# A fused linear attention and two MLPs on one core: the second MLP in five super blocks of 960 and 896 tokens and not in six of 768

## The chip, the core and the metric

The kernel runs on one core of a Trainium2 chip. The metric is the device time of one execution in microseconds (us), from the first to the last instruction with what lies around it. PE is the matmul engine, DVE, ACT and POOL are the three engines for elementwise work, SP issues nearly all DMAs. Each engine works through its own instructions in order; a semaphore makes one wait for another.

## The reference

The attention is linear: q is normalised over the head dimension, k over the sequence, and q is multiplied by the small matrix k'v of its head. Its output, 4608 tokens of 512, goes through two MLPs of width 2048.

```python
kv = einsum('bhsd,bhse->bhde', k_s, v)          # k_s: softmax of k over the sequence
attn = einsum('bhsd,bhde->bhse', q_s, kv)       # q_s: softmax of q over the head dimension
x = attn.transpose(0, 2, 1, 3).reshape(4608, 512)
h = x @ w_in;   x = maximum(h, 0) ** 2 @ w_out                    # first MLP
h = x @ w_in2;  out = (h / (1 + exp(-1.702 * h))) @ w_out2        # second MLP
```

## The kernel before

**Number format.** Every fp32 matmul is made of three with operands split in a high and a low part (`three`, L1193): high x high, high x low, low x high. The high part is a copy on ACT (L634), the low part a difference on POOL or DVE (L637).

**First part.** Attention and the first MLP run over nine blocks of 512 tokens, until about 867 us. Their matmuls are 512 columns wide, later (from the fourth block) a mix of 256 and 512.

**The second MLP** runs over `NB2` = 6 super blocks of 768 tokens. Both of its matrix products are made by a scheme of seven half-size products in place of eight (Winograd's form of Strassen's), so a super block is cut in two halves of `TH` = 384 tokens, and 384 is the width of all its matmuls. Each super block i does this:

- `steps_s` (L1456) loads the tokens into one tile (`xf`) and makes seven forms of it, a11, s2, a12, s3, s1, a22, s4: sums and differences of its quarters, each with high and low part. They lie in a ring of ten places, `X_PLACES` (L1422): three tiles of `xpool` and seven pairs or thirds of others.
- `steps_l1` (L1522) runs n = 8i to 8i + 7, with two blocks of 128 hidden units each. Every n has seven **products** of six matmuls, in the order a11, s2, a12, s3, s1, a22, s4, into two PSUM banks by turns. DVE and ACT take the results out, add, apply the activation and make seven forms of g (named ga and gs in the rows), with high and low parts.
- `chain` (L1659) is the second matrix product: for each pair of n, 14 **chains** of six matmuls. Those of five forms (pca, pcs) go into two PSUM banks by turns and are added by `evict` (L1689) on DVE to a sum in SBUF; two (pla, pls) stay in PSUM over the super block. The sums of a super block lie in a ring of eight places, `SUM_PLACES` (L1431).
- `steps_y` (L1707) combines the sums, turns them with DVE transposes into a tile of the same place as `xf`, and stores them.

On PE products and chains alternate, a product, a chain, a product; the chains lag by 11 products. So a "six" of one kind follows a six of the other, and a PSUM bank comes again after three others. The weights of the second MLP are read from DRAM anew in each super block (`load_in`, `load_out`).

**What sets the order.** Every step is planned with a time, but the order of nearly all steps is written out in the table `LATER` (names such as n15.a22 for a product, c98 for a chain, e98 for its eviction, b2.l.a22 for the low part of form a22 of super block 2, y1.o100 for a transpose). Each engine gets its instructions in that order.

Of the kernel before, what the change touches and what calls it, by code (L numbers as in the profile page):

```python
# [117 lines left out]
h7.h.s1 x31.wr x32.ld h7.l.s1 w0.b0 g2_4.hi h7.d.s1 w0.b1 g2_4.lo k31.bc m2_5 h7.h.s3 k31.sb r3_1.w1 w0.b2 k33.ld
k31.ex h7.l.s3 h7.u2 w1.ld s2_3 x31.rd h7.u3 g2_5.re h7.h.s2 g2_5.sq h7.l.s2 x32.mx g2_5.hi h7.d.s3 h7.h.a22 x32.sb
h7.d.s2 k31.kv g2_5.lo x32.ex m2_6 k33.vl k31.su x32.su k31.no h7.l.a22 k31.hi k33.mx k31.lo h7.d.a22 w1.ab x32.no  # L120
s2_4 r3_1.wq w1.b0 g2_6.re w1.b1 x31.hi f0.h.a11 x31.lo r3_1.wa f0.l.a11 g2_6.sq f0.h.a12 k32.tr m2_7 f0.l.a12
f0.d.a11 k32.m2 g2_6.hi w1.b2 f0.d.a12 g2_6.lo f0.u0 w2.ld f0.h.s4 x31.mm f0.l.s4 g2_7.re f0.u1 s2_5 x31.xe f0.d.s4
x32.tr a3.h.a11 g2_7.sq x32.wr a3.l.a11 x33.ld f0.u2 f0.h.s1 g2_7.hi k32.bc m2_8 f0.h.s3 g2_7.lo k32.sb f0.u3 k40.ld
k32.ex f0.l.s1 w2.ab f0.h.s2 f0.l.s3 s2_6 f0.d.s1 w2.b0 g2_8.re x32.rd f0.l.s2 w2.b1 g2_8.sq f0.d.s2 x33.mx k32.kv
g2_8.hi f0.d.s3 w2.b2 x33.sb m2_9 k40.mx w3.ld f0.h.a22 g2_8.lo x33.ex k32.su k32.no x33.su k40.vl f0.l.a22 k32.hi
x32.hi s2_7 g2_9.re x32.lo k32.lo f1.h.a12 g2_9.sq f0.d.a22 x33.no f1.h.a11 g2_9.hi k33.tr m2_10 g2_9.lo w3.ab k33.m2
w3.b0 a3.s3 w3.b1 x32.mm f1.l.a12 a3.h.s3 w3.b2 g2_10.re s2_8 x32.xe a3.l.s3 f1.d.a12 x33.tr f1.h.s4 w4.ld g2_10.sq
x33.wr f1.l.s4 x40.ld k33.bc g2_10.hi m2_11 k33.sb f1.l.a11 f1.d.s4 g2_10.lo k41.ld k33.ex f1.u0 f1.u1 s2_9 f1.u2
g2_11.re f1.d.a11 f1.u3 f1.h.s3 g2_11.sq f1.l.s3 w4.ab g2_11.hi w4.b0 f1.d.s3 k33.kv w4.b1 g2_11.lo x33.rd w4.b2 m2_12
f1.h.s2 k33.su k41.vl f1.l.s2 f1.h.s1 x40.mx k33.no k41.mx f1.l.s1 k33.hi s2_10 k33.lo g2_12.re x40.sb f1.d.s2  # L130
g2_12.sq w5.ld x40.ex x40.su x33.hi m2_13 g2_12.hi f1.d.s1 x33.lo x40.no g2_12.lo x33.mm g2_13.re s2_11 g2_13.sq
x33.xe a3.h.a12 x40.tr g2_13.hi a3.s1 a3.l.a12 x40.wr a3.h.a22 x41.ld a3.s2 a3.h.s1 m2_14 w5.ab g2_13.lo a3.s4 a3.h.s2
# [28 lines left out]
x50.su f3.d.s2 j3_6.s3 j3_6.r.c11 r4_0.w1 s3_9.2 x43.hi j3_6.+c22 x50.no s3_9.3 x43.lo j3_6.s1 j3_6.a22 r4_0.wa
j3_6.++c22 f3.h.a22 x43.mm f3.l.a22 r4_0.wq j3_6.+c21 f4.h.a11 s3_10.0 j3_6.r.c21 f4.l.a11 x50.tr j3_6.q.A s3_10.1
j3_6.h.A f4.u0 x50.wr j3_6.s4 f4.u1 x51.ld x43.xe j3_6.l.A s3_10.2 a4.h.a12 j3_6.++c12 r4_0.wb a4.s1 s3_10.3 j3_6.r.B
a4.l.a12 j3_6.q.B j3_7.a11 a4.s2 f3.d.a22 j3_7.s2 j3_7.m1 f4.d.a11 j3_6.h.B s3_11.0 j3_7.+c12 a4.h.a22 j3_6.l.B
s3_11.1 a4.s4 w10.ab j3_7.a12 f4.h.a12 f4.l.a12 j3_7.s3 x50.rd a4.l.a22 j3_7.r.c11 a4.h.s1 s3_11.2 a4.h.s2 a4.l.s1
s3_11.3 j3_7.+c22 f4.h.s4 a4.l.s2 r4_1.w1 j3_7.s1 f4.h.s1 f4.l.s4 j3_7.a22 r4_1.wa j3_7.++c22 x51.mx s3_12.0 f4.l.s1
r4_1.wq a4.h.s4 j3_7.+c21 s3_12.1 w10.b0 j3_7.r.c21 a4.l.s4 w10.b1 j3_7.q.A j3_7.s4 j3_7.h.A s3_12.2 r4_1.wb x51.sb
x50.hi s3_12.3 j3_7.++c12 w10.b2 j3_7.r.B j4_0.a11 f4.d.a12 j3_7.l.A f4.d.s4 j4_0.s2 x50.lo j4_0.m1 j3_7.q.B w11.ld
s3_13.0 j3_7.h.B s3_13.1 x51.ex j4_0.+c12 j3_7.l.B j4_0.a12 f4.u2 f4.d.s1 k50.tr j4_0.s3 r4_2.w1 j4_0.r.c11 k50.m2
s3_13.2 j4_0.+c22 f4.h.s3 x51.su s3_13.3 f4.l.s3 f4.h.s2 j4_0.s1 f4.u3 j4_0.a22 x51.no f4.d.s3 j4_0.++c22 r4_2.wa  # L170
# [1822 lines left out]
```

## Time and profile before

| | |
|---|---|
| median of 3 runs | 1585.75 us (1582.2 to 1586.27) |
| the profiled execution | 1584.51 us |
| its span, first to last instruction | 1582.6 us |
| PE busy | 1561.0 us |
| DVE, POOL, ACT busy | 1092.8, 991.9, 870.0 us |
| the second MLP's first product | at 867.19 us |

A busy PE in this profile is one that has a matmul under way; how fast it goes is read from the starts of its instructions. "Idle before" is the time an engine waited, with the instruction that released it.

### The profile page before, as it was taken

The page shows a single profiled execution, that of the slowest core. Times are in us where ns is not written, and L with a number is a line of the kernel's source. Part 1 is how long each engine was busy: PE and PEld are TensorE (multiplying, and loading weights), DVE is VectorE, ACT ScalarE, POOL GpSimd, SP SyncE. Part 2 cuts the span into 40 slices and gives each one's busy share as a digit, 9 for nine tenths or more (in the row PEclk, how much of TensorE's full clock was granted, in tenths as well). Part 3 has the DMA queues.
Part 4 walks back from the last instruction along what each step waited for, and adds up shares of the span by engine and source line. Part 5 has one row for each costly group of instructions (what it writes and reads, how often), then busy time and mean ns, then how long its engine had stood idle before and what let it go on. Part 6 is the DMA issues. An engine that isn't in the chain of part 4 may idle for free.

```text
span 1582.6 us, 26757 instructions
## 1 busy us (share of the span) xinstructions
PE 1561.0 (99%) x8996; PEld 1450.7 (92%) x8996; DVE 1092.8 (69%) x1762; ACT 870.0 (55%) x1723; POOL 991.9 (63%) x865
## 2 busy tenths in 40 slices
PE   7999999999999999999999999999999999999998
PEld 5888888899988988888899999999999999999997
DVE  8978868876868677676431556766767776677657
ACT  6774445556756766677544535545544544544442
POOL 6777766755756566676543556666667576576554
PEclk9999999999999999999999999999999999999999
DMA  9635659599999999989775677897987987887975
GB/s 276 214 122 173 199 173 289 163 299 309 318 302 322 324 300 332 306 292 322 235 271 165 221 247 251 281 309 247 283 313 244 282 311 252 277 300 263 283 255 163
DMA packets 260424, 414.93 MB, mean 262 GB/s; under 512 B 98496, under 2 KB 155840, under 8 KB 260288
## 3 DMA queue, kind: packets, MB, share of 16 engines
q1 hardware_dynamic: 254416, 409.03, 80.3%
q10 hardware_dynamic: 5872, 4.20, 0.9%
q8 instruction: 72, 1.18, 0.3%
q14 instruction: 64, 0.52, 0.1%
HBM read 342.88 MB, written 70.25 MB: 261 GB/s over the span
## 4 chain that ended last, share of the span: by engine, by line
PE 57%; DMA 2%; DVE 1%; ACT 1%; POOL 0%; issue 0%; SPq 0%; DVEq 0%; POOLq 0%; ACTq 0%
PE ps L1196 20%; PE pcs L1196 9%; PE pa L1196 8%; PE acc L1196 7%; PE pca L1196 6%; PE pla L1196 3%; PE pls L1196 3%; DMA wos<-outs 1%; DMA kt<-in_k_dram 0%; DMA q<-in_q_dram 0%; DMA rawo<-in_moe_w_out_dram 0%; DMA qd<-qd 0%; DVE o L1726 0%; PE px L1148 0%; PE pu L1196 0%
## 5 line engine op out<-in xcount | busy, mean ns | idle before, releaser
L1196 PE MATMUL acc<-g,wo 128*128 128x512 f32 x1728 | 440.4, 393 | 0.1
L1196 PEld LDWEIGHTS acc<-g,wo 128*128 128x128 f32 x1728 | 311.4, 189 | 54.9 <-DVE to L727 0.6
L637 POOL TENSOR_TENSOR ga<-c,ga 128x384 fp32r<-128x384 f32 x144 | 171.7, 1194 | 160.0 <-ACT ga L634 92.7
L1572 ACT ACTIVATE c<-c 128x384 f32<-128x384 f32 x144 | 75.6, 525 | 195.1 <-DVE c L1563 195.0
L637 POOL TENSOR_TENSOR g<-gs,g 128x512 fp32r<-128x512 f32 x72 | 99.7, 1385 | 112.8 <-ACT g L634 105.4
L1196 PE MATMUL pcs<-gs,ws 128*128 128x384 f32 x828 | 165.7, 334 | 0.0
L1563 DVE TENSOR_TENSOR c<-ps,m 128x384 f32<-128x384 f32 x144 | 79.7, 554 | 116.8 <-PE ps L1196 114.8
L637 POOL TENSOR_TENSOR gs<-s,gs 128x384 fp32r<-128x384 f32 x96 | 102.2, 1065 | 86.5 <-ACT gs L634 65.0
L1196 PEld LDWEIGHTS pcs<-gs,ws 128*128 128x128 f32 x828 | 145.5, 188 | 0.0
L1196 PE MATMUL ph<-x,wi 128*128 128x512 f32 x576 | 143.6, 397 | 0.3 <-ACT g L1217 0.2
L1196 PEld LDWEIGHTS ph<-x,wi 128*128 128x128 f32 x576 | 105.9, 188 | 24.1 <-issue 0.7
L637 POOL TENSOR_TENSOR gs<-c,gs 128x384 fp32r<-128x384 f32 x96 | 115.8, 1214 | 5.1 <-ACT gs L634 3.7
L1196 PE MATMUL pa<-a,w 128*128 128x384 f32 x576 | 115.4, 334 | 0.0
L1196 PE MATMUL ps<-s,wa 128*128 128x384 f32 x576 | 115.3, 334 | 0.0
L1196 PE MATMUL pca<-ga,wa 128*128 128x384 f32 x552 | 110.3, 334 | 0.0
L1196 PEld LDWEIGHTS pa<-a,w 128*128 128x128 f32 x576 | 101.3, 188 | 0.4
L1196 PEld LDWEIGHTS ps<-s,wa 128*128 128x128 f32 x576 | 101.3, 188 | 0.4
L1196 PEld LDWEIGHTS pca<-ga,wa 128*128 128x128 f32 x552 | 97.0, 188 | 0.0
L1705 DVE TENSOR_TENSOR sums<-pcs,sums 128x384 f32<-128x384 f32 x102 | 56.2, 554 | 46.1 <-PE pcs L1196 45.9
L1582 DVE TENSOR_TENSOR c<-c,c 128x384 f32<-128x384 f32 x96 | 84.1, 876 | 3.1 <-DVE c L1582 0.5
L1582 DVE TENSOR_TENSOR s<-c,c 128x384 f32<-128x384 f32 x96 | 77.4, 806 | 6.2 <-ACT c L1572 4.7
L634 ACT ACTIVATE gs<-s 128x384 fp32r<-128x384 f32 x96 | 50.5, 526 | 56.2 <-DVE s L1582 55.5
(216 smaller groups left out, 3558.1 us busy)
## 6 DMA issues: line engine op xcount, KB each, us to landing
ws<-wos SPq DMA_DIRECT2D x96, 512.0 KB, 4.2
wa<-woa SPq DMA_DIRECT2D x72, 512.0 KB, 4.8
w<-w1w SPq DMA_DIRECT2D x48, 512.0 KB, 5.3
wq<-w1wq SPq DMA_DIRECT2D x48, 512.0 KB, 6.0
wa<-w1wa SPq DMA_DIRECT2D x48, 512.0 KB, 5.7
w<-wiw SPq DMA_DIRECT2D x48, 512.0 KB, 4.5
wa<-wiwa SPq DMA_DIRECT2D x48, 512.0 KB, 4.6
wq<-wiwq SPq DMA_DIRECT2D x48, 512.0 KB, 5.1
```

Of the source, the lines that this page charges most:

```text
L634: nc.scalar.activation(hi, src, AF.Copy)
L637: eng.tensor_tensor(out=lo, in0=src, in1=hi.bitcast(F32), op=ALU.subtract)
L1196: nc.tensor.matmul(out, w(a), x(b), start=(start and e == 0), stop=(stop and e == 2), skip_group_check=shared)
L1563: nc.vector.tensor_tensor(out=st[name], in0=st[at][:, :TH], in1=other, op=ALU.add)
L1572: nc.scalar.activation(st[name], h, AF.Gelu_apprx_sigmoid)
L1582: nc.vector.tensor_tensor(out=st[out], in0=st[a], in1=st[b], op=op)
L1705: nc.vector.tensor_tensor(out=o, in0=bank, in1=o, op=ALU.add)
```

## The change

`TH` is no longer one number: `THS = (480, 480, 448, 448, 448)` gives the half of each of five super blocks (2 x 2304 = 4608 tokens). Matmuls, forms, g tiles, sums and stores of super block i take their width from it, and the planned times (`PTS`, `product_t`, `chain_t`) go by it. The forms now lie in eight places, each a pair of 4 KB tiles, the sums in six places of `xpool`, taken from a list as they come free, and three small tiles (m1, c22, c12) in the rest of those. The weight loads and the g tiles get other places of the same number. The table `LATER` is new, also for the steps of the first part. Diff, without the table:

```diff
-    TH = 384
+    THS = (480, 480, 448, 448, 448)
...
-    NB2 = NT // (2 * TH)
+    NB2 = len(THS)
+    T0 = [2 * sum(THS[:i]) for i in range(NB2)]
...
-    PT = 1.04
+    PTS = [6 * (n / 2.4 + 13.4) / 1000 for n in THS]
+    PT = max(PTS)
...
-    X_PLACES = ("x4", "x5", "x6", (0, 1), (2, 3), (4, 5), "x0", "x1", "x2", "x3")
+    X_PLACES = (
+        (places[7], places[8]), ("o3", "o4"), ("i0", "i1"), (places[9], "o0"), ("o1", "o2"), ("o5", "o6"), ("i2", "o10"), (held_x[5], held_x[6])
+    )
+    W_IN = dict(w1=("o8",), wa=("raw",), wb=("o9",), wq=("o7", "o12"))
+    W_OUT = ("o11", "i3", "i4", "i5")
+    G_PLACES = (*held_x[:5], "o13", "o14", "o15", "g4", "g5", "g6")
+    C_PLACES = dict(m1=("x4",), c22=("x5",), c12=("x6", "x0"))
+    sums_free = [f"x{1 + e}" for e in range(6)]
...
-    SUM_PLACES = (15, 16, 17, 18, None, 19, 20, 21)
...
     def steps_s(i):
         st = {}
+        TH = THS[i]
...
         if at == 0 and t == 0:
-            place = SUM_PLACES[(len(SUM_ORDER) * i + SUM_ORDER.index(x)) % len(SUM_PLACES)]
-            pool, tag = (cpool, "raw") if place is None else (wpool, slots[place])
-            totals[i, x] = pool.tile([P, 2, TH], F32, tag=tag, name=f"sum{x}_{i}")
+            place = sum_place[i, x] = sums_free.pop(0)
+            totals[i, x] = tile_at(place, TH, f"sum{x}_{i}", F32)
+            if x == "s1":
+                sums_free.extend(sum_place[i, e] for e in ("s2", "a22", "s3", "s1", "a11"))
...
-                times = [on(3, 9.0), on(4, 7.9), on(4, 9.75), on(5, 3.5), on(7, 5.5)]
-                times += [on(4, 11.5), on(4, 12.7), on(5, 5.0), on(5, 5.5), on(6, 6.5), on(6, 7.9)]
-                times += [on(7, 2.5), on(7, 3.0), on(7, 6.0), on(7, 7.9), on(7, 7.2), on(7, 8.0), e(3) + 0.2, on(7, 9.75)]
+                times = [on(3, 9.0), on(4, 7.9), on(4, 9.75), on(5, 3.5), e(1) + 1.8]
+                times += [on(4, 11.5), on(4, 12.7)]
+                for u in range(6):
+                    times += [e(u) + 0.2, e(u) + 1.4]
```

What the order has on PE where super block 1 (n = 15) meets super block 2 (n = 16), before (pca and pcs are chains, ps and pa products, x3 means three matmuls of one kind):

```order
L1196 MATMUL pca_99_12254<-ga_14_12050,wa_7_12088 128x384 x3
L1196 MATMUL pca_99_12254<-ga_15_12201,wa_7_12088 128x384 x3
L1196 MATMUL ps_15_12224<-s_1_10913,wb_12123 128x384
L1196 MATMUL ps_15_12224<-s_1_10914,wb_12123 128x384
L1196 MATMUL ps_15_12224<-s_1_10913,wb_12123 128x384 x2
L1196 MATMUL ps_15_12224<-s_1_10914,wb_12123 128x384
L1196 MATMUL ps_15_12224<-s_1_10913,wb_12123 128x384
L1196 MATMUL pca_100_12278<-ga_14_12091,wa_7_12139 128x384 x3
L1196 MATMUL pca_100_12278<-ga_15_12252,wa_7_12139 128x384 x3
L1196 MATMUL pa_16_12291<-a_2_11747,w_16_12197 128x384
```

and now:

```order
L1165 MATMUL pca_99_12212<-ga_14_11996,wa_7_12043 128x480 x3
L1165 MATMUL pca_99_12212<-ga_15_12154,wa_7_12043 128x480 x3
L1165 MATMUL ps_15_12178<-s_1_10939,wb_12077 128x480
L1165 MATMUL ps_15_12178<-s_1_10940,wb_12077 128x480
L1165 MATMUL ps_15_12178<-s_1_10939,wb_12077 128x480 x2
L1165 MATMUL ps_15_12178<-s_1_10940,wb_12077 128x480
L1165 MATMUL ps_15_12178<-s_1_10939,wb_12077 128x480
L1165 MATMUL pca_100_12239<-ga_14_12041,wa_7_12094 128x480 x3
L1165 MATMUL pca_100_12239<-ga_15_12210,wa_7_12094 128x480 x3
L1165 MATMUL pa_16_12250<-a_2_11581,w_16_12150 128x448
```

PE's sequence is the same; the widths differ, and from n = 16 products of 448 stand between chains of 480. Over the second MLP the rows count 4032 matmuls of 384 before, and 1344 of 480 and 2016 of 448 now.

On DVE in the same step (s_2 and a_2 are forms of super block 2 made from xf; the rows with pca are evictions, those with ps take out products), before:

```order
L637 TENSOR_TENSOR s_2_12165<-xf_11669,s_2_12165 128x768
L1563 TENSOR_TENSOR c_15_12186<-ps_15_12158,m_15_12152 128x384
L1563 TENSOR_TENSOR c_15_12218<-ps_15_12158,m_15_12152 128x384
L637 TENSOR_TENSOR a_2_12209<-xf_11669,a_2_12209 128x768
L1563 TENSOR_TENSOR c_15_12218<-ps_15_12224,c_15_12218 128x384
L1705 TENSOR_TENSOR suma_1_11266<-pca_98_12233,suma_1_11266 128x384
L1563 TENSOR_TENSOR c_15_12263<-ps_15_12158,m_15_12152 128x384
L1705 TENSOR_TENSOR suma_1_11266<-pca_99_12254,suma_1_11266 128x384
```

and now (lastingx are tiles of `xpool` that hold sums, m1, c22 and c12):

```order
L606 TENSOR_TENSOR s_2_12112<-xf_11511,s_2_12111 128x896
L1541 TENSOR_TENSOR lastingx_9001<-ps_15_12114,lastingx_9794 128x480
L1456 TENSOR_TENSOR xf_11511<-xf_11511 128x2x448
L1541 TENSOR_TENSOR lastingx_9838<-ps_15_12114,lastingx_9794 128x480
L606 TENSOR_TENSOR s_2_12163<-xf_11511,s_2_12162 128x896
L1541 TENSOR_TENSOR lastingx_9838<-ps_15_12178,lastingx_9838 128x480
L606 TENSOR_TENSOR a_2_12199<-xf_11511,a_2_12198 128x896
L1688 TENSOR_TENSOR lastingx_9810<-pca_98_12189,lastingx_9810 128x480
```

Three low parts and the difference for s4 now stand in this step, where two low parts stood, and the low part of a22 has moved to behind the third take-out, right ahead of the eviction of pca_98.

## Rows read from the trace of the kernel before

**Rows 1.** The page: the span and all its instructions.
```profile
span 1582.6 us, 26757 instructions
```
**Rows 2.** Busy time by stage: window, engines' busy us (instructions), PE clock, DMA.
```profile
100.00:720.00 620.00, 616.77 (x3574) 540.96 (x3574) 464.93 (x760) 379.67 (x761) 406.53 (x366) 1.00 0.85 268
...
890.00:1560.00 670.00, 670.00 (x3868) 670.00 (x3867) 457.39 (x698) 321.17 (x645) 422.67 (x349) 1.00 0.83 273
```
**Rows 3.** PE in order of time, second MLP: start us, us, what.
```profile
1012.05 1.20 PE L1196 MATMUL ps<-s,wq 128*128 128x384 f32 x6
1013.09 1.20 PE L1196 MATMUL pcs<-gs,ws 128*128 128x384 f32 x6
```
**Rows 4.** The same view where other widths stand, and at the opening.
```profile
94.77 0.37 PE L1148 MATMUL px<-qh,kvh 128*128 128x448 f32 x1
94.97 0.36 PE L1148 MATMUL px<-qh,kvl 128*128 128x448 f32 x1
...
219.72 2.88 PE L1196 MATMUL acc<-g,wo 128*128 128x512 f32 x12
222.44 2.88 PE L1196 MATMUL ph<-x,wi 128*128 128x512 f32 x12
...
867.19 1.23 PE L1196 MATMUL pa<-a,w 128*128 128x384 f32 x6
868.25 0.86 PE L1196 MATMUL acc<-g,wo 128*128 128x512 f32 x3
868.95 1.22 PE L1196 MATMUL ps<-s,wq 128*128 128x384 f32 x6
```
**Rows 5.** PE, then DVE, in order of time at the kernel's end.
```profile
1562.20 2.24 PE L1196 MATMUL pva<-ga,wa 128*128 128x384 f32 x12
...
1576.54 0.58 DVE L1726 STREAM_TRANSPOSE o<-suma 128x384 f32<-128x384 f32 x1
...
1577.59 0.58 DVE L1726 STREAM_TRANSPOSE o<-suma 128x384 f32<-128x384 f32 x1
```
**Rows 6.** Groups by line and shape: count, busy us, mean ns, idle before.
```profile
L1563 DVE TENSOR_TENSOR c<-ps,m 128x384 f32<-128x384 f32 x144 | 79.7, 554 | 116.8 <-PE ps L1196 114.8 <-ACT gs L634 1.3 <-POOL gs L637 0.6
L1368 DVE TENSOR_TENSOR misc<-ps,misc 128x256 f32<-128x256 f32 x96 | 40.3, 419 | 58.9 <-PE ps L1196 53.5 <-ACT misc L1363 5.0
L637 POOL TENSOR_TENSOR ga<-c,ga 128x384 fp32r<-128x384 f32 x144 | 171.7, 1194 | 160.0 <-ACT ga L634 92.7 <-PE ps L1196 26.0 <-PE pcs L1196 20.5
L637 POOL TENSOR_TENSOR g<-g,g 128x512 fp32r<-128x512 f32 x48 | 64.3, 1341 | 25.8 <-ACT g L634 25.2
```
**Rows 7.** Two windows of one n each, and the groups that make forms.
```profile
995.40:1010.00 14.60, 14.60 (x86) 14.60 (x86) 13.96 (x23) 7.22 (x16) 10.20 (x8) 1.00 0.78 260
...
1082.80:1097.30 14.50, 14.50 (x85) 14.50 (x84) 10.25 (x15) 8.99 (x17) 12.53 (x10) 1.00 0.74 260
...
L637 DVE TENSOR_TENSOR s<-xf,s 128x768 fp32r<-128x768 f32 x12 | 16.2, 1350 | 2.6 <-ACT s L634 2.6
L637 DVE TENSOR_TENSOR a<-xf,a 128x768 fp32r<-128x768 f32 x6 | 12.0, 2008 | 1.0 <-PE acc L1196 1.0
L1473 DVE TENSOR_TENSOR xf<-xf 128x768 f32<-128x768 f32 x6 | 8.3, 1386 | 0.0
...
L637 POOL TENSOR_TENSOR a<-xf,a 128x768 fp32r<-128x768 f32 x12 | 24.1, 2007 | 2.5 <-ACT a L634 2.5
L637 POOL TENSOR_TENSOR s<-xf,s 128x768 fp32r<-128x768 f32 x6 | 14.7, 2450 | 1.0 <-ACT s L634 1.0
L637 POOL TENSOR_TENSOR s<-s1f,s 128x768 fp32r<-128x768 f32 x6 | 11.1, 1849 | 0.0
...
L634 ACT ACTIVATE a<-xf 128x768 fp32r<-128x768 f32 x18 | 14.6, 835 | 5.4 <-DMA xf<-y 2.9 <-PE acc L1196 1.7 <-DVE s2x L637 0.8
```
**Rows 8.** SP and ACT in order of time: an input load and its first reader.
```profile
1039.80 1.20 SPq L1466 DMA_DIRECT2D xf<-y x2
...
1047.82 1.58 ACT L634 ACTIVATE a<-xf 128x768 fp32r<-128x768 f32 x2 [2.22 <-DMA xf<-y]
```

More of the change, by code (lines that the diff above doesn't have):

```diff
@@ L118 @@
[L118 to L132, printed above, removed]
@@ L135 @@
+x40.tr f1.d.s1 g2_13.hi a3.s1 a3.l.a12 x40.wr a3.h.a22 x41.ld a3.s2 a3.h.s1 m2_14 g2_13.lo a3.s4 a3.h.s2 w5.ab a3.l.s1
+s2_12 a3.l.s2 g2_14.re a3.h.s4 x40.rd a3.l.s4 g2_14.sq m2_15 settle a3.l.a22 g2_14.hi x41.mx f1.h.a22 g2_14.lo
+f2.h.a11 w5.b0 f2.h.a12 s2_13 x41.sb r3_0.wb g2_15.re w5.b1 r3_1.wb r3_2.wb f1.l.a22 x40.hi g2_15.sq x41.ex j3_0.a11
 f2.l.a11 f1.d.a22 x40.lo j3_0.s2 j3_0.m1 f2.l.a12 f2.d.a11 g2_15.hi s2_14.0 j3_0.+c12 x41.su s2_14.1 g2_15.lo f2.d.a12
@@ L161 @@
[L161 to L170, printed above, removed]
@@ new lines @@
+n13.l.a22 c85 v15.wq n13.+c21 n13.a.c21 n13.s4 l6.s1 e85 n13.s3' c86 n13.s1' v14.wb n13.h.s3 n13.++c12 n13.h.s1
+n13.l.s3 n14.a11 n13.s2' n13.a.c12 n13.h.a12 n13.l.s1 c87 e86 n14.m1 n13.s4' n13.h.s2 n13.l.a12 n14.s2 l6.s4 e87
+n13.h.s4 c88 n13.l.s2 n14.+c12 n14.a12 n13.l.s4 e88 c89 v15.w1 n14.a.c11 n14.h.a11 n14.s3 l6.a12 e89 n14.l.a11 c90
+n14.+c22 n14.s1 e90 c91 v15.wa n14.++c22 n14.a.c22 n14.a22 n14.h.a22 l7.a11 e91 n14.l.a22 c92 v16.wq n14.+c21
+n14.a.c21 n14.s4 n14.s3' n14.s1' n14.h.s3 c93 v15.wb n14.++c12 n14.h.s1 n14.l.s3 n14.s2' n14.a.c12 n15.a11 n14.h.a12
@@ new lines @@
+n20.l.s3 n21.a11 n20.s2' l10.a22 n20.h.s1 n20.h.a12 c136 n20.l.s1 n21.m1 e135 n20.h.s2 n20.s4' n21.s2 n20.l.s2
+n20.h.s4 c137 n21.+c12 n20.l.a12 n21.a12 l10.s3 n20.l.s4 c138 v22.w1 n21.a.c11 n21.h.a11 n21.s3 n21.l.a11 c139
+n21.+c22 n21.s1 l10.s2 c140 v22.wa n21.++c22 n21.a.c22 n21.a22 n21.h.a22 e140 n21.l.a22 c141 v23.wq n21.+c21 n21.a.c21
+n21.s4 l10.s1 e141 n21.s3' c142 n21.s1' v22.wb n21.h.s3 n21.++c12 n21.h.s1 n21.l.s3 n22.a11 n21.s2' n21.a.c12
+n21.h.a12 n21.l.s1 c143 e142 n22.m1 n21.s4' n21.h.s2 n22.s2 n21.l.a12 l10.s4 e143 n21.h.s4 c144 n21.l.s2 n22.+c12
@@ L514 @@
+n39.s1 l19.s3 n38.l.s4 c266 n39.++c22 n38.l.a12 n39.a.c22 n39.a22 n39.h.a22 e266 n39.l.a22 c267 n39.+c21 n39.a.c21
+n39.s4 l19.s1 n39.s3' n39.s1' e267
 """
@@ L548, in shift_key @@
         return f"{kind}{'n' if n == 3 else ''}.{step}"
-    alone = dict(b=n < 2, v=n < 2, l=n < 1, y=n == 5)
-    if kind not in alone:
+    alone = dict(b=n < 2, v=n < 2, l=n < 1, y=n == 4)
+    if kind not in alone or (kind == "b" and n):
         return None
@@ L1421, with lasting, tile_at @@
     X_ORDER = ("a11", "s2", "a12", "s3", "s1", "a22", "s4")
-    X_PLACES = ("x4", "x5", "x6", (0, 1), (2, 3), (4, 5), "x0", "x1", "x2", "x3")
     held = len(FORMS) * (NB - 1 - NAT)
     places = [X1_PLACES[(held + e) % len(X1_PLACES)] for e in range(len(X1_PLACES))]
-    slots = places[len(FORMS) :] + [f"o{f}" for f in range(NF - 3)] + [f"i{e}" for e in range(6)] + places[: len(FORMS)]
-    slots += [f"o{f}" for f in range(NF - 3, NF)]
-    W_IN = dict(w1=(6,), wa=(7,), wb=(8,), wq=(9, 10))
-    W_OUT = (11, 12, 13, 14)
+    held_x = places[: len(FORMS)]
+    X_PLACES = (
[6 more added lines that the diff above has]
+    sums_free = [f"x{1 + e}" for e in range(6)]
+    lasting_x = {}
+    def lasting(tag):
+        if tag not in lasting_x:
+            lasting_x[tag] = xpool.tile([P, 3 * TB], F32, tag=tag, name=f"lasting{tag}")
+        return lasting_x[tag]
+    def tile_at(tag, width, name, dtype=F32R):
+        if tag[0] == "x":
+            return lasting(tag)[:, : 2 * width].rearrange("p (k c) -> p k c", k=2)
+        pool = cpool if tag == "raw" else late["pool"] if tag[0] == "g" else wpool
+        return pool.tile([P, 2, width], dtype, tag=tag, name=name)
     SUM_ORDER = ("a11", "a22", "s3", "s2", "s1")
-    SUM_PLACES = (15, 16, 17, 18, None, 19, 20, 21)
     def g_tile(x, n):
@@ L1733, in run @@
             def run():
-                r0, c = (2 * i + row) * TH, col * HC + 64 * q
+                r0, c = T0[i] + row * TH, col * HC + 64 * q
                 (nc.scalar if q % 2 and i == NB2 - 1 else nc.sync).dma_start(
@@ L1773 @@
         grid = opening + 11 * (PT + UNIT) + UNIT
-        SLOT = 2.09
+        SLOT = 2 * PT + 0.01
         last = NQ * NB2 * 7 - 11
+        chain_t, product_t = [], []
+        t = grid
+        for c in range(NQ * NB2 * 7 + NX):
+            product_t.append(t)
+            if c < last:
+                t += PTS[(c + 11) // 7 // NQ] + 0.01
+            chain_t.append(t)
+            t += PTS[min(c // (NX * GROUPS), NB2 - 1)]
         def product_at(n, e):
             at = 7 * (n - 1) + e - 4
-            return opening + (PT + UNIT) * (7 * n + e) if at < 0 else grid + SLOT * at
+            return opening + (PT + UNIT) * (7 * n + e) if at < 0 else product_t[at]
         def chain_at(c):
-            return grid + SLOT * min(c, last) + PT * (1 + max(c - last, 0))
-        g_free = {at: 0.0 for at in range(22, 2 * NF)}
+            return chain_t[c]
+        g_free = {at: 0.0 for at in G_PLACES}
         unit_at = [opening + (PT + UNIT) * (e + 1) - UNIT + 0.01 for e in range(11)] + [grid - UNIT + 0.01]
         ends = [t + UNIT for t in unit_at[NC - 1 :: NC]]
-        g_free.update({29: ends[0], 30: ends[1], 31: ends[2]})
-        g_free["g4"] = 0.0
+        g_free.update(o13=ends[0], o14=ends[1], o15=ends[2])
         g_three = list(ends)
```

757 lines of the change are left out of this document (366 added, 391 removed).

## The prediction

> **What bounds the kernel now.** I read the page first, for the span [rows 1], then the busy time by stage, then PE's own order of time. By stage the granted clock is 1.00 in both windows, the 2.4 GHz level; from 890 to 1560 us PE is busy 670.00 of 670.00 us, while DVE has 457, ACT 321 and POOL 423; from 100 to 720 us 3.2 us are missing [rows 2]. The view of who PE waited for has no entry from 890 to 1560. So in the second MLP nothing but PE's own rate sets the time, and the question is what one matmul costs there.
>
> In PE's order of time a product or a chain is six matmuls of 384 columns, and a new six starts every 1.04 us [rows 3]: 173.3 ns a matmul, where 384 columns at 2.4 GHz are 160.0. So 13.3 ns go with the matmul and not with its columns. Other widths agree: twelve of 512 take 222.44 - 219.72 = 2.72 us, 226.7 each, 13.3 over 213.3; 448 columns start 0.20 us apart, 13.3 over 186.7 [rows 4].
>
> **The matmuls of the second MLP.** The order counts 4032 matmuls of 384 columns before, and 1344 of 480 with 2016 of 448 after: the same columns, 672 matmuls fewer. I cut the sum where the last product ends, since what follows is not paced by PE alone: 72 matmuls stand behind it, 12 chains of six; the first of them starts where that product ends, at 1562.20 [rows 5]. Before: (4032 - 72) x 173.3 ns = 686.4 us. After: 1344 x (200.0 + 13.3) = 286.7 and (2016 - 72) x 200.0 = 388.8, together 675.5. That is **-10.9 us**. The width 480 stands in no row; it lies between 448 and 512. By the clean 512 row it is 213.3; its bad end is the 512 that stands among narrower ones: 700 ns for three, 233 each, so 6.6 ns more than clean [rows 4].
>
> **Where widths mix.** At the opening six of 384 beside three of 512 take 1.76 us [rows 4] where 1.04 + 0.68 was due, 0.04 more. The opening keeps this mix. New is one place, block 1 to block 2, where 448-wide products alternate with the last eleven or so 480-wide chains: 11 x 0.04 = **+0.4 us**, bounds 0 and 0.4 (384 beside 384 shows none).
>
> **The tail.** From the end of the last product, 1562.20, to the end of the last transpose, 1577.59 + 0.58 = 1578.17, are 16.0 us, and DVE's last pairs of add and transpose end 1.05 us apart [rows 5]. All of it gets 448 columns for 384. A DVE add from PSUM is 554 ns at 384 and 419 at 256, so 1.05 ns a column: +67 ns, 12%. POOL's low parts go from 1194 at 384 to 1341 at 512, +6% for 64 columns; PE's matmul goes +15% [rows 3, 4, 6]. DVE is last there, so 16.0 x 0.12 = **+1.9 us**, bounds 1.0 and 2.4. From the last transpose to the span's end are 4.4 us of output stores [rows 1, 5]; they carry a sixth more: 0 to +0.7, I take **+0.3**.
>
> **What costs nothing.** The second MLP's weights are read five times and not six. Those 1/6 fewer loads stand in SP's queue beside a PE that never waits there, so they give nothing by themselves. The per-column work of DVE, ACT and POOL is the same in sum and comes in fewer instructions; PE's unit grows from 1.04 to 1.28 or 1.20 us, 23% and 15%, a DVE add by 18% and 12%, so cover grows in the steady part. The next block's input load waits for the last output store out of the same tile, and the form a11 that reads it stands seven sixes behind it in both orders (block 1 to 2). Before, that ACT instruction waited 2.2 us for the load [rows 8], and PE lost nothing. Now the load is 960 or 896 tokens for 768: 8.0 us from issue to reading become at most 10.0, seven sixes 9.0 us for 7.3, so the wait becomes 2.2 + 2.0 - 1.7 = 2.5 us: 0, and at most those 0.3 us once.
>
> **The order of the first part.** PE's order up to the first product of the second MLP is the same row for row; on the other engines many steps are moved by a place or two. PE's waits there are 3.2 us in all [rows 2]: at best they vanish, at worst I let them double. **0, bounds -3.2 and +3.2.**
>
> **The smaller rings.** The x forms had ten places and now have eight, the sums eight and now six. With eight places, six of the seven forms of the next block can be written only as the products of the block's last step free their places. On DVE that step now holds three low parts and a difference of the next block where it held two low parts (the order shows it). Window 1082.8 to 1097.3 is that step before: DVE 10.25, POOL 12.53 us of 14.5 [rows 7]. DVE without its two forms (1.35 + 2.01) is 6.9; at 480 columns 6.9 x 1.18 = 8.1, and the new four (2 x 1.35 + 2.01 + 1.39 = 6.1 at 768) x 1.25 = 7.6: 15.7 of 17.9 us. POOL without its two (1.85 + 2.45) is 8.2; by 9% more 9.0, and three forms (1.85 + 2.45 + 2.01) x 1.25 = 7.9: 16.9 of 17.9 us. Both fit, POOL barely. The tightest place is the a11 chain that follows product s1 (pca_98 in the order). DVE reaches its eviction only after the low part of form a22. From the end of product s1: ACT's high part 0.84 x 1.25 = 1.0, DVE's low part 2.01 x 1.25 = 2.5, the eviction 0.65: 4.2 us. The chain ends 1.28 after s1 and its bank is wanted three units later, at 5.1. So 0.9 us are left, and I take **0**. The sums' places are freed by the output transposes at least two chains ahead of their next writer.
>
> **Sum.** -10.9 + 0.4 + 1.9 + 0.3 = -8.3 us. The profiled execution took 1584.51 us (its span 1582.6 and 1.9 around it), 1.24 below the median of 1585.75 and inside the runs' 1582.2 to 1586.27. 1584.5 - 8.3 = **1576.2 us**.
>
> **Rivals.**
> (1) *The rings bite.* The place is the step above, four times in a run (blocks 0 to 1 up to 3 to 4). Every us by which the eviction comes later than the 0.9 us left is a us of PE. It gives the gain back at 8.3 / 4 = 2.1 us of wait each, 3.0 us of lateness. For it: POOL is full there, and DVE's low part of a22 ran 2.01 us against 1.35 for the other forms, so it is the one that suffers beside POOL. Against it: before, a fuller window of DVE, 13.96 of 14.6 us, cost PE nothing [rows 7]. A wait of 1 us each gives 1580.2; of 2.1, 1584.5; of 3, 1588.2.
> (2) *Wide matmuls cost more.* If 480 and 448 columns pay, like the 512 among narrower ones, 6.6 ns more, it is 3288 x 6.6 ns = 21.7 us: 1597.9, **slower**. It decides from 8.3 / 3288 = 2.5 ns a matmul. For it: the 233 ns. Against it: the 512 among 512 and the 448 show none, and apart from one place the widths are uniform after the opening.
> (3) *The count is free.* If a matmul costs by its columns and 13.3 ns were only this kernel's pairs of tiles, the 672 save nothing and only mix and tail stay: 1584.5 + 2.6 = 1587.1, **no change**. Three widths speak against it. The Trainium skill has such a rule: "TensorE: Matmul & The Clock Gate", section "Wait — 56ns, not 53.3ns?", gives N / 2.4 GHz plus about 2.5 ns for warm matmuls back to back; by that figure an estimate of the saving is 672 x 2.5 ns = 1.7 us, and the time 1585.4. The trace does not agree with it here: it has 13.3 ns [rows 3, 4].
> (4) *The first part gets worse.* +3.2 us and more in the moved steps: 1579.4, up to 1582.
> That the change does not do what it says is excluded: the order shows the widths and counts.
>
> **Chances.** Forecast 0.72. (1) 0.13, of it 0.04 faster, 0.05 no change, 0.04 slower. (2) 0.06, slower. (3) 0.03, no change. (4) 0.06, half faster, half no change. So faster by over 0.3% 0.79, within 0.3% 0.11, slower 0.10; 0.3%, 4.8 us, is about what a measurement of this kernel can tell from no change. Range: down by the 3.2 us of waits to 1573, and up over (4) and the small end of (1) to 1583.
>
> **What would show it.** The step between two sixes should read 1.28 us in blocks 0 and 1 and 1.20 in blocks 2 to 4. PE busy should equal the window from the opening to the last product, with an empty list of waits: a wait of PE on DVE or POOL at a block's end is (1). A step of 1.31 or more is (2). PE's waits between 100 and 720 us above 3.2 are (4). The tail from the last product to the span's end should read 22.6 us for 20.4. The forecast is wrong if 480 columns have a price of their own, or if the four crossings wait by over 1 us each.

## The result, and the profile after

| kernel | median, us | lowest to highest | ratio to the kernel before, beside it |
|---|---|---|---|
| before | 1585.47 | 1582.20 to 1586.27 | |
| changed | 1596.01 | 1594.55 to 1597.83 | 1.0063, interval 1.0051 to 1.0075 |
| changed, measured once more | 1593.37 | 1589.48 to 1594.35 | 1.0051, interval 1.0033 to 1.0068 |

The change makes the kernel slower by 0.5 to 0.6%. The forecast was 1576.2 us, faster, in a range of 1573 to 1583.

The page of the changed kernel begins with its span and the instructions of each engine; the windows are those of [rows 2].

```profile
span 1595.7 us, 24796 instructions
...
PE 1570.5 (98%) x8324; PEld 1384.0 (87%) x8324; DVE 1070.7 (67%) x1638; ACT 857.2 (54%) x1610; POOL 983.8 (62%) x803
...
100.00:720.00 620.00, 614.77 (x3556) 539.02 (x3556) 458.30 (x754) 377.89 (x756) 401.79 (x363) 1.00 0.84 264
...
890.00:1560.00 670.00, 670.00 (x3182) 596.96 (x3181) 431.98 (x572) 306.02 (x537) 410.24 (x288) 1.00 0.72 228
```

In the second MLP PE is busy 670.00 of 670.00 us at a granted clock of 1.00, as in [rows 2]. Everything around it got lighter: the mean share of the DMA engines went from 0.83 to 0.72, VectorE from 457 to 432 us, and 3182 matmul records stand where 3868 stood. The rings do not bite. The list of what PE waited for, from the first product of the second MLP to the end, holds two entries, both in the tail; its columns are who waited, for whom, us in total, times, longest.

```profile
PE pu L1165 <- POOL gs L606: 0.4, 1, 0.4
PE pvs L1165 <- DVE lastingx L1677: 0.2, 1, 0.2
```

So the time is in PE's own rate. PE in order of time, neighbouring sixes of 480 columns and of 448, which answer to [rows 3]:

```profile
1001.81 1.46 PE L1165 MATMUL ps<-s,wa 128*128 128x480 f32 x6
1003.10 1.46 PE L1165 MATMUL pla<-ga,wa 128*128 128x480 f32 x6
1004.40 1.46 PE L1165 MATMUL ps<-s,wa 128*128 128x480 f32 x6
...
1399.87 1.40 PE L1165 MATMUL pca<-ga,wa 128*128 128x448 f32 x6
1401.11 1.40 PE L1165 MATMUL pa<-a,w 128*128 128x448 f32 x6
1402.35 1.40 PE L1165 MATMUL pca<-ga,wa 128*128 128x448 f32 x6
```

A six of 480 starts every 1.295 us where 1.28 was forecast, a six of 448 every 1.24 us where 1.20 was forecast. From the starts of the single matmuls, over all neighbours of one width, the mean is 216.3 ns at 480 (single steps 210 to 226) and 206.67 ns at 448 (a steady 207, 207, 206). At 2.4 GHz that is the width and 39 cycles, and the width and 48 cycles, where 384 columns have the width and 32.

### The profile page after: what moved, and what is told of

Same layout as the page of the kernel before. It is cut to its first block, busy times and chain, and to the rows that moved or that the text cites. A ratio compares the mean times of both kernels' runs of the same rounds, so it can differ in the third digit from the quotient of the medians.

```text
span 1595.7 us, 24796 instructions
## 1 busy us (share of the span) xinstructions
PE 1570.5 (98%) x8324; PEld 1384.0 (87%) x8324; DVE 1070.7 (67%) x1638; ACT 857.2 (54%) x1610; POOL 983.8 (62%) x803
## 4 chain that ended last, share of the span: by engine, by line
PE 85%; DMA 7%; DVE 4%; ACT 3%; issue 1%; POOL 1%; SPq 0%; DVEq 0%; ACTq 0%; POOLq 0%
PE ps L1165 23%; PE acc L1165 19%; PE pa L1165 9%; PE pcs L1165 9%; PE ph L1165 7%; PE pca L1165 6%; PE pls L1165 3%; PE pla L1165 3%; PE pk L968 2%; DMA qd<-qd 1%; PE px L1117 1%; DMA q<-in_q_dram 1%; DMA rawo<-in_moe_w_out_dram 1%; DMA rawi<-in_moe_w_in_dram 1%; DMA wiwa<-outs 1%
## 5 line engine op out<-in xcount | busy, mean ns | idle before, releaser
L1541 DVE TENSOR_TENSOR lastingx<-ps,lastingx 128x448 f32<-128x448 f32 (+1 forms) x160 | 101.2, 632 | 143.7 <-PE ps L1165 103.6
L606 POOL TENSOR_TENSOR ga<-lastingx,ga 128x448 fp32r<-128x448 f32 (+1 forms) x80 | 112.1, 1402 | 135.7 <-ACT ga L603 95.1
L1165 PE MATMUL pcs<-gs,ws 128*128 128x448 f32 (+1 forms) x684 | 162.6, 372 | 0.0
L606 POOL TENSOR_TENSOR gs<-s,gs 128x448 fp32r<-128x448 f32 (+1 forms) x80 | 103.5, 1294 | 90.5 <-ACT gs L603 61.4
L606 POOL TENSOR_TENSOR gs<-c,gs 128x448 fp32r<-128x448 f32 (+1 forms) x80 | 119.9, 1511 | 2.1 <-ACT gs L603 1.9
L1165 PE MATMUL pa<-a,w 128*128 128x448 f32 (+1 forms) x480 | 114.0, 372 | 0.0
L1165 PE MATMUL ps<-s,wa 128*128 128x448 f32 (+1 forms) x480 | 114.0, 372 | 0.0
L1165 PE MATMUL pca<-ga,wa 128*128 128x448 f32 (+1 forms) x456 | 108.2, 372 | 0.0
L1688 DVE TENSOR_TENSOR lastingx<-pcs,lastingx 128x448 f32<-128x448 f32 (+1 forms) x84 | 52.6, 634 | 46.2 <-PE pcs L1165 46.2
L606 POOL TENSOR_TENSOR g<-g,g 128x512 fp32r<-128x512 f32 x48 | 66.0, 1376 | 26.7 <-ACT g L603 25.6
```

The costliest lines, as they stand in the source:

```text
L606: eng.tensor_tensor(out=lo, in0=src, in1=hi.bitcast(F32), op=ALU.subtract)
L1165: nc.tensor.matmul(out, w(a), x(b), start=(start and e == 0), stop=(stop and e == 2), skip_group_check=shared)
L1541: nc.vector.tensor_tensor(out=st[name], in0=st[at][:, :TH], in1=other, op=ALU.add)
L1688: nc.vector.tensor_tensor(out=o, in0=bank, in1=o, op=ALU.add)
```

## The experiments

**The price of a width by itself.** If a wide matmul is dear here, it may be for its width, for where its operand lies, or for the work around it. The kernel `e0_widths` leaves all of that work out. In its sections `n` every operand lies from column 0, in `k` the operands are packed, in `p` padded to multiples of 512 columns; in `mix` sixes of two widths alternate; in `w` the weights change with every six, in `v` with every matmul:

```diff
+    for n in (256, 320, *range(384, 513, 8)):
+        section(f"n{n}x", (n,), (0,))
...
+    section("k448x", (448,), (0, 896, 0, 448, 1344, 448))
+    section("p448x", (448,), (0, 1024, 0, 512, 1536, 512))
...
+    section("mixax", (448, 480), (0,), 96)
+    section("mixbx", (384, 512), (0,), 96)
+    for n in (384, 448, 480, 512):
+        section(f"w{n}x", (n,), (0,), 48, lambda e: e // 6 % 16)
+        section(f"v{n}x", (n,), (0,), 48, lambda e: e % 16)
```

> The price of one matmul by its width, measured by itself: the attention, both MLPs and all their work are left out; the kernel only loads random data and runs chains of six FP32r products of 128 x 128 weights back to back into two banks, in sections of eight sixes each. Sections differ in the width (256, 320, 384 to 512 by 8), in where the second operand lies (all from column 0; at the columns 2n, n, 3n as in the changed kernel, or at 1024, 512, 1536), in alternating widths, and in whether the weights change. Theory A, the price goes by the width: start to start is the width and 32 cycles at 2.4 GHz at 256, 384 and 512 (120.0, 173.3, 226.7 ns), and more than that at 448 and 480 wherever the operand lies: 206.7 and 216.3 ns as in the changed kernel, not 200.0 and 213.3. Theory B, it goes by where the operand lies, a row of 448 or 480 columns behind another starting off some boundary: 200.0 and 213.3 ns with all operands from column 0 and at 512, 1024, 1536, and 206.7 and 216.3 ns at n, 2n, 3n. Theory C, it comes from the work around the matmuls in the kernel (ScalarE, VectorE and DMA on the same memory): 200.0 and 213.3 ns in every section here.

PE in order of time; each row is a section of 48 matmuls (the `mix` ones 96), so the step from one row's start to the next row's, divided by 48, is the price of one:

```profile
53.40 8.48 PE L52 MATMUL n384x<-xs,ws 128*128 128x384 f32 x48
61.72 8.67 PE L52 MATMUL n392x<-xs,ws 128*128 128x392 f32 x48
...
96.72 9.28 PE L52 MATMUL n424x<-xs,ws 128*128 128x424 f32 x48
105.84 9.56 PE L52 MATMUL n432x<-xs,ws 128*128 128x432 f32 x48
115.24 9.76 PE L52 MATMUL n440x<-xs,ws 128*128 128x440 f32 x48
124.84 9.90 PE L52 MATMUL n448x<-xs,ws 128*128 128x448 f32 x48
134.57 10.19 PE L52 MATMUL n456x<-xs,ws 128*128 128x456 f32 x48
...
164.86 10.58 PE L52 MATMUL n480x<-xs,ws 128*128 128x480 f32 x48
175.28 10.99 PE L52 MATMUL n488x<-xs,ws 128*128 128x488 f32 x48
...
207.73 11.07 PE L52 MATMUL n512x<-xs,ws 128*128 128x512 f32 x48
218.63 8.51 PE L52 MATMUL k384x<-xs,ws 128*128 128x384 f32 x48
...
235.30 10.08 PE L52 MATMUL k448x<-xs,ws 128*128 128x448 f32 x48
245.21 10.08 PE L52 MATMUL p448x<-xs,ws 128*128 128x448 f32 x48
255.13 10.63 PE L52 MATMUL k480x<-xs,ws 128*128 128x480 f32 x48
265.60 10.57 PE L52 MATMUL p480x<-xs,ws 128*128 128x480 f32 x48
276.01 20.37 PE L52 MATMUL mixax<-xs,ws 128*128 128x448 f32 x96
296.22 19.63 PE L52 MATMUL mixbx<-xs,ws 128*128 128x384 f32 x96
315.69 8.48 PE L52 MATMUL w384x<-xs,ws 128*128 128x384 f32 x48
...
332.33 10.08 PE L52 MATMUL w448x<-xs,ws 128*128 128x448 f32 x48
342.24 10.08 PE L52 MATMUL v448x<-xs,ws 128*128 128x448 f32 x48
352.16 10.56 PE L52 MATMUL w480x<-xs,ws 128*128 128x480 f32 x48
362.56 10.56 PE L52 MATMUL v480x<-xs,ws 128*128 128x480 f32 x48
372.96 11.09 PE L52 MATMUL w512x<-xs,ws 128*128 128x512 f32 x48
```

| columns | 384 | 424 | 432 | 440 | 448 | 456 | 480 | 488 | 504 | 512 |
|---|---|---|---|---|---|---|---|---|---|---|
| measured, ns | 173.3 | 190.0 | 195.8 | 200.0 | 202.7 | 209.0 | 217.1 | 225.6 | 227.1 | 227.1 |
| width and 32 cycles, ns | 173.3 | 190.0 | 193.3 | 196.7 | 200.0 | 203.3 | 213.3 | 216.7 | 223.3 | 226.7 |

Up to 424 columns a matmul costs its width and 32 cycles, within 1.7 ns; above, it costs 2 to 9 ns more, and at 512 it is back at 32 cycles. 504 columns cost what 512 do. Where sixes of 384 and 512 alternate (`mixbx`), a matmul takes 202.8 ns in the mean where the two prices give 200.0: the 512s pay it, at 231.5 ns, so they are not cheap between sixes of 384. Nothing runs beside PE here, so Theory C falls: the work around is not the cause. Packed and padded operands cost nearly the same, 206.5 and 206.7 ns at 448, 218.1 and 216.9 at 480, so Theory B falls as an explanation of the price. Theory A holds, with one thing it did not have: 448 has two prices, 202.7 ns in the section `n448x` and 206.7 in `k448x` and `p448x`. In the first the single steps repeat 199, 207, 203, 202, 203; in the second each is 206 or 207. I call them the cheap and the dear rhythm. No section of 448s ran at 200.0.

**Padded places in the changed kernel.** The same widths, each form in a place of 512 columns (the last pair of lines moves m1, c22 and c12, which PE does not read):

```diff
-            return gpool.tile([P, 2, THS[n // NQ]], F32R, tag="g", name=f"g{x}_{n}")
+            return gpool.tile([P, 2, 512], F32R, tag="g", name=f"g{x}_{n}")[:, :, : THS[n // NQ]]
-        return tile_at(at, THS[n // NQ], f"g{x}_{n}")
+        return tile_at(at, 512, f"g{x}_{n}")[:, :, : THS[n // NQ]]
...
-                st["x", a] = [tile_at(at, TH, f"{a}{e}_{i}") for e, at in enumerate(place)]
+                st["x", a] = [tile_at(at, 512, f"{a}{e}_{i}")[:, :, :TH] for e, at in enumerate(place)]
...
-                return lasting(at[n % len(at)])[:, 2 * max(THS) : 2 * max(THS) + TH]
+                return lasting(at[n % len(at)])[:, 1024 : 1024 + TH]
```

> The changed kernel, widths unchanged (480, 480, 448, 448, 448), but every x form and g form stands in a place that is 512 columns wide, so that the second row of a form, and so each operand, starts at a multiple of 512 columns. Theory A (width): no change, sixes 1.297 and 1.240 us apart and 1596 us. Theory B (where the operand lies): sixes 1.28 and 1.20 us apart, 17.5 us less between the first and the last product, 1578.5 us. Theory C (the work around): no change.

1587.52 us, between the two forecasts. In the trace the 480s are unchanged (216.7 ns), and the 448s stand 202.7 ns apart: the cheap rhythm. 1944 matmuls of 448 up to the last product times 4.0 ns are 7.8 of the 8.5 us by which this run is under 1596.0. So neither theory's numbers came: the layout did not bring 200.0 and 213.3, but it changed the rhythm. Is that the layout's doing, or the luck of one execution?

> The same program as the padded run: the widths of the changed kernel, each operand at a multiple of 512 columns. In that run, which took 1587.5 us, the 448s were 202.7 ns apart in a repeated pattern (199 to 207), where the changed kernel has a steady 206.7. Theory E, where the operands lie sets which of the two rhythms a 448 falls into: again 202.7 ns and 1587.5 us in all executions. Theory F, the rhythm is a matter of how the chain of matmuls was entered, by chance in each execution: some executions at 1587 and some at 1596 us, and the profile may show 206.7.

1589.17 us (1584.33 to 1591.17; ratio to before 1.0006, interval 0.9994 to 1.0017), and in the new trace 202.7 ns again, from the first 448s to the end. Here are its sixes of 448, 1.216 us apart where the changed kernel's are 1.240:

```profile
1399.60 1.38 PE L1165 MATMUL pcs<-gs,ws 128*128 128x448 f32 x6
1400.82 1.38 PE L1165 MATMUL ps<-s,wa 128*128 128x448 f32 x6
1402.03 1.38 PE L1165 MATMUL pcs<-gs,ws 128*128 128x448 f32 x6
```

In two profiles of one program the rhythm is the same, so it belongs to the program and not to the execution. The changed kernel, profiled once more, agrees:

> The changed kernel as it is, once more: if the 206.7 ns of its 448s belong to the program, again 206.7 in the profile and 1596 us; if they came by chance in one execution, 202.7 and 1588 us. The first product of the second MLP, at 872.6 us in its first profile, comes by 867 to 870 us, as in five kernels with the same first part, if the 3 us more were chance.

1593.37 us, 206.67 ns at 448 and 216.3 at 480, as in its first profile. The second half of the expectation, on the first part, came too, at 869.11 us:

```profile
869.11 1.46 PE L1165 MATMUL pa<-a,w 128*128 128x480 f32 x6
```

**What sets the rhythm.** `e7_entry` runs 24 matmuls of some width, and then 48 of 448 or 480 in three layouts (`s` all from column 0, `k` packed, `p` padded):

> Chains of six FP32r products by themselves again, attention, MLPs and all their work left out: 48 products of 448 or 480 columns behind 24 of 256, 384, 440, 464, 488 or 512, with all operands at column 0, packed (at 2n, n, 3n) or at multiples of 512 columns. Theory E (where they lie): the rhythm of the 448s, 206.7 or about 202.6 ns, differs between the layouts and not by the width ahead. Theory F (how they are entered): it differs by the width ahead and not by the layout. Neither expects 200.0 ns at 448 or 213.3 at 480, the width and 32 cycles.

PE in order of time, the second number is the section's us; 9.9 is the cheap rhythm, 10.08 the dear one:

```profile
57.98 10.08 PE L52 MATMUL s448from384x<-xs,ws 128*128 128x448 f32 x48
72.70 10.07 PE L52 MATMUL s448from440x<-xs,ws 128*128 128x448 f32 x48
...
118.18 9.89 PE L52 MATMUL s448from512x<-xs,ws 128*128 128x448 f32 x48
...
144.70 10.07 PE L52 MATMUL k448from384x<-xs,ws 128*128 128x448 f32 x48
159.42 9.89 PE L52 MATMUL k448from440x<-xs,ws 128*128 128x448 f32 x48
...
204.40 9.89 PE L52 MATMUL k448from512x<-xs,ws 128*128 128x448 f32 x48
```

All sections of 448, us, by the width ahead:

| layout | 256 | 384 | 440 | 464 | 488 | 512 |
|---|---|---|---|---|---|---|
| `s` | 9.89 | 10.08 | 10.07 | 10.08 | 9.89 | 9.89 |
| `k` | 9.89 | 10.07 | 9.89 | 9.90 | 9.90 | 9.89 |
| `p` | 9.89 | 10.07 | 10.07 | 10.08 | 9.89 | 9.89 |

In one and the same layout the width ahead makes a difference: behind 256, 488 and 512 all three layouts are cheap, behind 384 all three are dear. Behind 440 and 464 it is the layout: packed is cheap, the other two are dear. So Theories E and F are each half right: the rhythm is taken up at the start of a stretch, what ran ahead and how the operands lie both change it, and then it is kept. These two do not settle it alone: `n448x` in `e0_widths`, from column 0 and behind 440 too, was cheap (9.90), where `s448from440x` is dear (10.07); 48 matmuls of 440 stood ahead there and 24 here, and other sections before those. And 480, the width that stands ahead of the 448s in the changed kernel, is not among the widths ahead here. The 480s stay between 216.5 and 218.4 ns in every section. Why a stretch locks into one rhythm or the other is not shown by any of these runs.

In the full kernel the width ahead was tried with a first block of 512 and packed places, `THS = (512, 448, 448, 448, 448)`:

> The changed kernel with halves of 512, 448, 448, 448 and 448, forms packed as in it. If the packed places (theory E) give the dear rhythm: 672 x 226.8 + 2688 x 206.65 = 707.9 us where the changed kernel has 707.4: 1596.5 us. If it goes by what ran before the 448s (theory F; here 512s, there 480s), 202.7 ns are to be had: 697.2 us, 1586 us.

1586.21 us in one execution, with the 448s at 202.7 ns throughout: Theory F's number. The packed places did not keep the cheap rhythm away, as they should have done by Theory E.

**Other widths, the same columns, the same count of matmuls.** Without a 448:

```diff
-    THS = (480, 480, 448, 448, 448)
+    THS = (480, 480, 480, 480, 384)
```

> The changed kernel with halves of 480, 480, 480, 480 and 384: no block of 448 is left, as many matmuls over as many columns, the order as it is. Theory A (width): 2688 x 216.3 + 672 x 173.3 = 697.9 us for 707.4, and a tail 1.8 us shorter: 1584.7 us, about the kernel before. Theory C or B with the 448s as dear as the 480s (both 5 ns over the width and 32 cycles): 2688 x 218.3 + 672 x 173.3 = 703.2, 1590 us.

1582.85 us in one execution, 1.9 below Theory A's 1584.7; 216.2 ns at 480 and 173.3 for most of the 384s. So the 448 is the worse of the change's two widths: 6.7 ns above its width and 32 cycles in the changed kernel, where the 480 is 3.0 above. And with 512 and 384 alone, the two that cost their width and 32 cycles:

```diff
-    THS = (480, 480, 448, 448, 448)
+    THS = (512, 512, 512, 384, 384)
```

> The changed kernel with the five super blocks in halves of 512, 512, 512, 384 and 384 tokens and not 480, 480, 448, 448, 448; the order is left as it is. There are as many matmuls (3360) over as many columns. Theory A (448 and 480 are dear widths, 384 and 512 cost the width and 32 cycles): 2016 x 226.7 + 1344 x 173.3 = 689.9 us where the changed kernel pays 2016 x 206.7 + 1344 x 216.3 = 707.4, and a tail that is some 1.8 us shorter, its last block being 384 wide again: 1596.0 - 17.5 - 1.8 = 1576.7 us, faster than both kernels, if no new wait comes from the order. Theory B (wherever an operand starts): 512 and 384 lie on boundaries too, the same 1576.7. Theory D, everything wider than 384 pays some 6.7 ns (512 at 233, as in the mixed rows of the first part): 2016 x 233.3 + 1344 x 173.3 = 703.3, so 1590 us.

1579.96 us, 0.9950 of the kernel before (interval 0.9931 to 0.9970). The 512s stand 226.8 ns apart, their width and 32 cycles: Theory D falls. The profiled execution took 1582.23 us, 5.5 above the expected 1576.7. Some 4.2 of these are a wait of 2.3 us at 1388 us and the matmuls behind it, some ten of 320 ns each at a granted clock of 0.50, the 1.2 GHz level, from 1391 to 1394 us (PE in order of time; then a window with PE's busy us, its granted clock, the DMA share and GB/s):

```profile
1390.90 2.26 PE L1165 MATMUL ps<-s,wa 128*128 128x384 f32 x6 [2.26 <-DMA wa<-wiwa]
...
1391.00:1394.00 3.00, 3.00 (x10) 0.50 1.04 418
```

A second measurement:

> Halves of 512, 512, 512, 384, 384 once more, for its own interval beside the run with the moved load: 1580 us, between 1575 and 1582, the wait at 1388 us again in the profile if it belongs to the order and not to one execution.

1577.63 us, 0.9948 of the kernel before (0.9935 to 0.9961): **faster than both kernels**. The wait is there again, shorter:

```profile
1387.05 1.21 PE L1165 MATMUL pcs<-gs,ws 128*128 128x384 f32 x6
1389.14 1.30 PE L1165 MATMUL ps<-s,wa 128*128 128x384 f32 x6 [0.88 <-DMA wa<-wiwa]
1390.28 1.20 PE L1165 MATMUL pcs<-gs,ws 128*128 128x384 f32 x6
```

Two tries to take that wait away, by which block is narrow and by the order:

```diff
-    THS = (512, 512, 512, 384, 384)
+    THS = (384, 512, 512, 512, 384)
```

> Halves of 384, 512, 512, 512 and 384 tokens: the same widths as in the run before with 512, 512, 512, 384, 384, in which one load of weights came 2.3 us late to TensorE at 1388 us, in the first 384s behind a 512 block, where the stores of one block of 1024 tokens and the load of the next x stand ahead of it. With a 384 block first and one last, each store of a block and each load of an x lies under a 512 block. Theory A (512 and 384 are cheap widths, the rest of that run was the late load and the clock that was low after it): the wait goes, 1579.96 - 2.3 - about 1.8 = 1575.9 us. Rival: the order, which is left as it was planned for other widths, gives a new wait at the first crossing, and it stays at 1580 us or above.

1582.13 us (ratio 0.9975, 0.9957 to 0.9993): the rival. The late load is gone, and at the first crossing PE waits 1.69 us for an eviction of VectorE instead. The profiled execution took 1579.83 us, and this wait is 1.7 of the 3.9 us by which it is over the expected 1575.9; what the slower executions add, up to 1592.12 us, is not shown.

```profile
983.04 1.31 PE L1165 MATMUL pca<-ga,wa 128*128 128x384 f32 x6 [1.69 <-DVE lastingx L1688]
```

In the other, block 4's load and its first two readers are moved back in the order:

```diff
-... n27.l.a11 b4.ld c181 ... v28.wb n27.h.s3 ... n27.l.a12 b4.h.a11 l13.s4 ... c187 b4.s1 v29.w1 ... n28.h.a11 n28.s3 ... n28.l.a11 c188
+... n27.l.a11 c181 ... v28.wb b4.ld n27.h.s3 ... n27.l.a12 l13.s4 ... c187 v29.w1 ... n28.h.a11 b4.h.a11 n28.s3 ... n28.l.a11 b4.s1 c188
```

> Halves of 512, 512, 512, 384, 384, with three steps of block 4 moved in the order: the load of its x (1.5 MB, on SP's queue) from ahead of the weights wa, wq and wb of step 28 to behind them, and the first split and the first sum that read it (ScalarE and GpSimd) to behind the first split of step 28. Theory A (the late load of wa at 1388 us was the x load ahead of it on the DMA engines): TensorE's wait of 2.3 us and the low clock behind it go, about 4 us of the plain 512-384 version, so 1576 us beside its 1580. Rival: the transfers only change places, another load of weights comes late, and the time stays.

1580.75 us (0.9979, 0.9963 to 0.9995), 3.1 above the 1577.63 of the order left as it was, measured beside it: the rival in its time, but not in its reason. No load of weights comes late. The x comes later to its readers: ScalarE waits 2.2 us for it, GpSimd 1.1; VectorE stands idle for 3.2 us and starts its own step on the x, at 1398.80 us, as GpSimd's third one ends (1398.77). PE waits for an add of VectorE behind that step:

```profile
1398.00 1.21 PE L1165 MATMUL pcs<-gs,ws 128*128 128x384 f32 x6
1401.06 1.54 PE L1165 MATMUL pa<-a,w 128*128 128x384 f32 x6 [1.86 <-DVE c L1541]
```

An order planned for these widths was not tried.

## Why the prediction was wrong, point by point

**What bounds the kernel: right.** PE's rate sets the second MLP before and after; PE is busy in the whole window.

**The matmuls: the wrong step.** The term was 1344 x 213.3 + 1944 x 200.0 = 675.5 us. Measured are 1344 x 216.3 = 290.7 and 1944 x 206.67 = 401.8, so 17.0 us more: 13.0 from the 448s and 4.0 from the 480s. From the first product to the end of the last one the kernel before took 1562.20 - 867.19 = 695.0 us, the changed one takes 1573.47 - 872.62 = 700.9, so +5.8 where -10.9 + 0.4 was forecast. These 16.3 us are most of the miss in the two measurements: +10.5 and +8.2 for -8.3, so 18.8 and 16.5.

Two readings failed. The 200.0 at 448 came from one pair of starts in [rows 4], printed to 10 ns (205 ns in the trace), in a stretch of the first part where other such pairs lie 195 to 211 ns apart, with a mean of 203. And the 213.3 at 480 was laid on a line between 448 and 512: the constant over the width was the same 32 cycles in three rows, at 384, 448 and 512, but one of these three rows was not good enough to stand for a point, and the line bends between 424 and 512.

**Where widths mix: small, of the other sign.** Where sixes of 448 and 480 alternate, the step from a 448 to a 480 is 207 ns and from a 480 to a 448 214, no more than among themselves. So of the 0.7 us left over (17.0 for 16.3) 0.4 are the cost forecast here that did not come; the other 0.3 is the kernel before, whose 3960 matmuls of 384 take 686.65 us, 173.4 ns each, where 686.4 was reckoned.

**The tail: right.** From the end of the last product to the span's end the kernel before took 20.4 us, the changed one takes 1595.7 - 1573.47 = 22.2: +1.8, forecast +2.2. VectorE's pairs of add and transpose end 1.19 us apart for 1.05, as priced; the start of the chains behind the last product and of the last two transposes, in answer to [rows 5]:

```profile
1573.47 2.64 PE L1165 MATMUL pva<-ga,wa 128*128 128x448 f32 x12
...
1589.17 0.65 DVE L1710 STREAM_TRANSPOSE o<-lastingx 128x448 f32<-128x448 f32 x1
...
1590.36 0.65 DVE L1710 STREAM_TRANSPOSE o<-lastingx 128x448 f32<-128x448 f32 x1
```

A VectorE add takes 618 ns at 448 columns and 653 at 480, as the 1.05 ns a column of [rows 6] have it (621 and 655):

```profile
L1541 DVE TENSOR_TENSOR lastingx<-ps,lastingx 128x448 f32<-128x448 f32 x96 | 59.4, 618 | 76.4 <-PE ps L1165 61.2 <-POOL ga L606 15.1
L1541 DVE TENSOR_TENSOR lastingx<-ps,lastingx 128x480 f32<-128x480 f32 x64 | 41.8, 653 | 67.3 <-PE ps L1165 42.5 <-POOL ga L606 24.8
```

**The first part: right within what can be told.** In the first profile PE misses 5.2 us between 100 and 720 us, above the 3.2 that were to show rival (4), and the first product stands at 872.62 for 867.19. But in nine later profiles, of this kernel and of those that differ from it in the second MLP alone, it stands between 866.7 and 871.5, and 2.6 to 6.9 us are missing. The 5.4 us of the first profile are mostly that one execution; a cost of 1 or 2 us of the new order can't be told from none.

**The rivals.** (1), the rings, fell: no wait of PE at any crossing of the changed kernel, though VectorE made its four forms there as the order showed (7.2 us in all from block 1 to 2, where 7.6 was reckoned). In the runs with 512 and 384 there are waits of PE on a load or on VectorE, in a narrow block or right at its end. (2) came nearest, with 1597.9 us, slower. Its 6.6 ns a matmul are what the 448s pay (6.67), but in a uniform stretch, where the rival had them from widths that mix; the 480s pay 3.0, so the matmuls give 17.0 of its 21.7 us, and that its time is within 2 us of the median is in part luck. It got a chance of 0.06 because 448 seemed measured, and its sign was looked for in the wrong place: the step of 1.31 us that was to show it was set for the 480s alone, which read 1.295, while the 448s had no mark. (3), that the count is free, fell with `e0_widths`, where some 13.3 ns go with each matmul at 256, 384 and 512 columns, and with the 512-384 version: it has the same columns and 672 matmuls fewer than the kernel before, and takes 703.0 us from the first product to the end of the last chain for 709.6 (second measurement, its wait included). The Trainium skill's figure that rival went by ("TensorE: Matmul & The Clock Gate", section "Wait — 56ns, not 53.3ns?", the width and some 2.5 ns) is met by no width here; the nearest are 13.3 ns over the width.

The idea of the change, fewer and wider matmuls, was sound, and so was its sum's form. It failed on the choice of the two widths.

## What to carry to other kernels

Before an even split chooses a new tile width, measure that width, alone and in a long uniform stretch; a constant that fits two widths need not hold between them, and a price taken from one pair of starts is no price. Where PE's rate is the bound, an uneven split into widths that are cheap (here 512 and 384) can beat an even one into widths that are not (480 and 448), with the same columns and the same count. Part of what such a split gives was given back here in waits in the narrow blocks or at their end, under an order planned for other widths; whether an order planned for these would take the waits away is not shown.
